# Two chained MLPs after a DFT on one Trainium2 core: operands shifted by 32 bytes, PSUM pools kept across the change of stage, the last flush and the last product done differently

## Chip, core and metric

One NeuronCore of a Trainium2 chip (trn2). The metric is the device time of one execution in microseconds, smaller is better. TensorE is called PE here, its weight loads PEld, VectorE DVE, ScalarE ACT, GpSimd POOL, SyncE SP.

## What is computed

```python
X = np.fft.fft(np.fft.fft(x, axis=1), axis=2).real        # x: 4 x 3072 x 256, float32
h = X.reshape(-1, 256) @ w_in                              # 12288 x 2048
y = np.maximum(0.01 * h, h) @ w_out                        # first MLP, 12288 x 256
y_prev = y shifted by one token inside each batch
xk = mu_k * y + (1 - mu_k) * y_prev;  xr = the same with mu_r
k = np.maximum(xk @ w_k, 0.0)                              # 12288 x 1024
out = sigmoid(xr @ w_r) * ((k * k) @ w_v)                  # second MLP
```

The weights arrive as float64 and are split on the chip. Precision is kept by writing each operand as a high part and a low part in `fp32r` and adding three products, high x high, high x low and low x high: so one mathematical matmul is three on PE.

## The kernel before

**Two stages.** The tokens are cut into 24 tiles of 512 (4 batches, 2 halves by symmetry of the DFT, 3 tiles each). The first stage does, for every batch, the DFT along the sequence by cosine and sine tables (`fft_mm`, line 309) and the first MLP; the DFT along the 256 columns is folded into `w_in` at the start (line 401). Its results `y` go to DRAM. The second stage reads them back as `xa` and, shifted by one token, `xb` (`load_tile`, line 671) and does the second MLP, tile after tile. The order of all work is written out by hand: each engine runs its instructions in the order in which the Python code issues them.

**First MLP.** For each of 16 slices `u` of the 2048 hidden columns (`step`, line 592) PE does 3 matmuls `mm_b` (line 508), 3 `mm_a` for the next slice (line 496), both into a PSUM tile of pool `ps_s` (tag `s`, 4 banks), and 12 matmuls `outmm` (line 519) into the four banks of pool `ps_o` (tags `o00` to `o11`): 18 matmuls of 128x128 stationary and 512 moving columns per slice. At the last slice of a tile `flush` (line 522) copies the four banks on ACT into two SBUF tiles `yo` of pool `work` and sends each to DRAM.

**The change of stage (lines 942 to 963).** The first two hidden slices of tile 0 of the second MLP are computed early out of `stage` tiles. Then the pools `work`, `pqp`, `mv`, `wp` (SBUF) and `ps_o`, `ps_s` (PSUM) are released, and `p2` (SBUF) and `ps2` (PSUM) take their space. The first user of a place in a new pool waits for everything that still uses the old pool there.

**Second MLP (lines 1014 to 1054).** For each tile and each of 8 hidden slices `f`: 6 matmuls `kps` (line 932), relu on ACT (`rl`, line 936), square on DVE (line 937), split into `k2h` and `k2l`, and two slices later 6 matmuls `v` (line 975) into two banks. In two of the slices 6 matmuls `rps` (line 983) feed the sigmoid. So a tile has 8 x 6 + 8 x 6 + 2 x 6 = 108 matmuls. Meanwhile the operands of the next tile are made: `mt` on ACT (line 688), `mx` on DVE (line 689), then the split `mh` (ACT, line 128) and `ml` (DVE, line 135). These six steps begin at slice `f1` of the tile before, one step per slice:

```python
        f0, f1, g0 = (0, 2, 4) if ti else (2, 5, 5)
```

At the end of a tile `finish` (line 987) multiplies gate and `v` on DVE and stores the two halves `m`; for the last tile each half is stored by itself.

**Where the operands lie.** All pools start on fixed byte offsets inside a partition of SBUF; every matmul's moving operand is a row of 512 x 4 = 2048 bytes there, its stationary operand a row of 512 bytes. `w2p` (the second MLP's weights) is allocated from the right end, `wp`, `mv`, `p2` and others from the left, after `misc`. As the built program places them, the start addresses modulo 64 bytes are:

```
matmuls                       moving operand        stationary operand     moving, stationary mod 64
first MLP, o (line 519)       gh 93056, gl 117632   uoh 76672, uol 84864   0, 0
first MLP, ps (496, 508)      Ph 101248, Qh 109440  wh 43904, wl 60288     0, 0
second MLP, kps (932)         mh 109504, ml 117696  wkh 192480             0, 32
second MLP, v (975)           k2h 64448, k2l 70592  wvh 208864             0, 32
second MLP, tile 0, kps       mh 20608 (in stage)   wkh 192480             0, 32
DFT (309)                     tables from 201568    sh 222176, sl 223712   0, 8, 32, 40, 48, 56; 32
dps (540), 2 weight columns   wh, wl                dcs 43520 or 43552     0, 0 or 32
```

Of the kernel before, what the change touches and what calls it, by code (L numbers as in the profile page):

```python
# [9 lines left out]
F32 = mybir.dt.float32  # L10
# [3 lines left out]
ALU = mybir.AluOpType  # L14
PSUM = bass.MemoryType.PSUM
DRAM = bass.MemoryType.DRAM

P = 128
B = 4
# [6 lines left out]
NK = FK // P  # L26
J = 384
JP = 386
W = 512
NT = M // W  # L30
# [72 lines left out]
def fft_mlp_kernel(ctx, tc, xs, x7, x8, x87, tb, tbs, alt, ce, so, mu, w_in, w_out, w_k, w_v, w_r, out):  # L103
    nc = tc.nc
    ctx.enter_context(tc.manual_schedule())
    V, A, T, G, Q = nc.vector, nc.scalar, nc.tensor, nc.gpsimd, nc.sync

    dram = ctx.enter_context(tc.tile_pool(name="dram", bufs=1, space=DRAM))
    yd = [[dram.tile([P, 2, M], F32, name=f"y{b}_{s}") for s in range(2)] for b in range(B)]
# [4 lines left out]
    ps_s = tc.alloc_tile_pool(name="ps_s", bufs=4, space=PSUM)  # L114
    ps_o = tc.alloc_tile_pool(name="ps_o", bufs=1, space=PSUM)
    stage = ctx.enter_context(tc.tile_pool(name="stage", bufs=3))
    misc = ctx.enter_context(tc.tile_pool(name="misc", bufs=1))
    x87t = misc.tile([1, 2, 4], F32, name="x87t")
    w128 = misc.tile([P, NF], F32, name="w128")
    wp = tc.alloc_tile_pool(name="wp", bufs=1)  # L120

    mv = tc.alloc_tile_pool(name="mv", bufs=1)
# [397 lines left out]
                     start=(u == 0 and i == 0), stop=(u == NF - 1 and i == 2))  # L520

    def flush(b, t, po):
        for s in range(2):
            yo = work.tile([P, 2, W], F32, tag="yo", bufs=2, name="yo")
            for h in range(2):
                act_copy(yo[:, h], po[s][h])
            Q.dma_start(yd[b][s][:, :, t * W:(t + 1) * W], yo)
# [136 lines left out]
    for n in range(len(sources)):  # L664
        a, c = w2_piece(n)
# [288 lines left out]
    pqp.release()  # L954
    mv.release()
    wp.release()
    ps_o.release()
    ps_s.release()


    ps2 = ctx.enter_context(tc.tile_pool(name="ps2", bufs=1, space=PSUM))
    p2 = w2["p2"] = ctx.enter_context(tc.tile_pool(name="p2", bufs=2))
    p2.tile([P, 16], F32, tag="pad", bufs=1, name="pad3")

    NB = D // P

    def v_mm(f, kk, vps):
        hi, lo = kk
        ws = ((w2["vh"], hi), (w2["vl"], hi), (w2["vh"], lo))
        order = [(i, m) for i in range(3) for m in range(NB)]  # L970
        if f == NK - 1:
            order = [(i, m) for m in range(NB) for i in range(3)]
        for i, m in order:
            w, x = ws[i]
            T.matmul(vps[m], w[:, f, m * P:(m + 1) * P], x, start=(f == 0 and i == 0), stop=(f == NK - 1 and i == 2))  # L975

    def r_mm(xr, sig, m):
        hi, lo = xr
        ps = ps2.tile([P, 512], F32, tag="rps", bufs=2, name="rps")
        i = 0  # L980
        for w, x in ((w2["rh"], hi), (w2["rl"], hi), (w2["rh"], lo)):
            for k in range(2):
                T.matmul(ps, w[:, k, m * P:(m + 1) * P], x[:, k], start=(i == 0), stop=(i == 5))  # L983
                i += 1
        A.activation(sig[:, m], ps, ACTF.Sigmoid)

    def finish(ti, vps, sig):
        o = p2.tile([P, NB, W], F32, tag="o", name="o")
        for m in range(NB):
            V.tensor_tensor(o[:, m], sig[:, m], vps[m], op=ALU.mult)  # L990
            if ti == len(tiles) - 1:
                Q.dma_start(out[ti, :, m], o[:, m])
        if ti < len(tiles) - 1:
            Q.dma_start(out[ti], o)

# [6 lines left out]
    def drain():  # L1002
        if q2:
            t, f, kk = q2.pop(0)
            if f == 0:
                t["v"] = [ps2.tile([P, 512], F32, tag="v", bufs=4, name=f"v{m}") for m in range(NB)]
            v_mm(f, kk, t["v"])
            if f == NK - 1:
                finish(t["i"], t["v"], t["sig"])

# [4 lines left out]
    for ti in range(len(tiles)):  # L1015
        rd = ready.pop(ti)
        t = {"i": ti, "sig": p2.tile([P, NB, W], F32, tag="sig", name="sig")}
        end = ti == len(tiles) - 1
        f0, f1, g0 = (0, 2, 4) if ti else (2, 5, 5)
        if ti == 0:  # L1020
            q1.append((t, 1, early[1][2]))
            q2.append((t, 0, kk0))
        for f in range(f0, NK):
            ps = ps2.tile([P, 512], F32, tag="k", bufs=2, name="kps")
            r = p2.tile([P, W], F32, tag="r", bufs=3, name="rl")
            k2 = p2.tile([P, W], F32, tag="k2", bufs=3, name="k2")
            k_mm(ps, f, rd["k"])
            k_ev(ps, r, k2)
            if q1:
                tt, ff, kk2 = q1.pop(0)  # L1030
                q2.append((tt, ff, k_split(kk2)))
            q1.append((t, f, k2))
            t["rk"] = rd.get("r")
            if not end and g0 <= f < g0 + NB:
                gate(t, f - g0)
            if end and f == NK - 1:
                gate(t, 0)
            if len(q2) > 1:
                drain()
            if f == f0:  # L1040
                for n in ((1, 2) if ti == 0 else (ti + 2,)):
                    if n < len(tiles):
                        loaded[n] = load_tile(n)
            if f == f1 and not end:
                for g in todo:
                    g()
                todo = do_prep(ti + 1)
            if todo:
                todo.pop(0)()
# [4 lines left out]
    drain()  # L1054
    for k in ("xp", "pool"):
        w2[k].release()


def dft_tables():
# [73 lines left out]
```

## Time and profile before

| | |
|---|---|
| median of 3 runs | 1498.52 us (1498.14 to 1502.74) |
| the profiled execution, its own time | 1498.63 us |
| its span, first to last instruction | 1496.9 us |
| PE busy | 1479.1 us, 99% of the span |
| PEld busy | 1203.2 us, 80% |
| DVE busy | 1008.2 us, 67% |
| ACT busy | 893.0 us, 60% |
| POOL busy | 124.2 us, 8% |
| granted TensorE clock | full (2.4 GHz) in all 40 slices of the span |

The profiled execution took 1.7 us more than its span. Matmuls overlap in the pipe, so the time that a matmul is listed with (390 ns) is its passage and not what it costs: what it costs is the distance from its start to the next start. A busy share of 99% for PE therefore says that PE always had something in flight, not that it ran at its peak.

### The profile page before, as it was taken

The page shows a single profiled execution, that of the slowest core. Times are in us where ns is not written, and L with a number is a line of the kernel's source. Part 1 is how long each engine was busy: PE and PEld are TensorE (multiplying, and loading weights), DVE is VectorE, ACT ScalarE, POOL GpSimd, SP SyncE. Part 2 cuts the span into 40 slices and gives each one's busy share as a digit, 9 for nine tenths or more (in the row PEclk, how much of TensorE's full clock was granted, in tenths as well). Part 3 has the DMA queues.
Part 4 walks back from the last instruction along what each step waited for, and adds up shares of the span by engine and source line. Part 5 has one row for each costly group of instructions (what it writes and reads, how often), then busy time and mean ns, then how long its engine had stood idle before and what let it go on. Part 6 is the DMA issues. An engine that isn't in the chain of part 4 may idle for free.

```text
span 1496.9 us, 17655 instructions
## 1 busy us (share of the span) xinstructions
PE 1479.1 (99%) x6460; PEld 1203.2 (80%) x6460; DVE 1008.2 (67%) x1409; ACT 893.0 (60%) x1473; POOL 124.2 (8%) x145
## 2 busy tenths in 40 slices
PE   6999999999999999999999999999999999999998
PEld 3788888888888888888888877888888888888887
DVE  7886767666666766676767656666666666666664
ACT  4776566565665665665666656555555555555563
POOL 2333000222000221000000000000000000000000
PEclk9999999999999999999999999999999999999999
DMA  8767132654141751232220111212121212121200
GB/s 318 216 180 131 32 114 91 203 111 83 36 156 62 200 99 36 68 124 92 89 68 0 57 64 64 85 42 85 43 84 43 85 43 78 50 71 57 71 29 29
DMA packets 88449, 134.23 MB, mean 90 GB/s; under 512 B 31342, under 2 KB 51575, under 8 KB 84778
## 3 DMA queue, kind: packets, MB, share of 16 engines
q1 hardware_dynamic: 73098, 86.50, 18.1%
q0 software_dynamic: 15264, 46.60, 12.6%
q8 instruction: 50, 0.82, 0.2%
q14 instruction: 37, 0.30, 0.1%
HBM read 105.20 MB, written 27.89 MB: 89 GB/s over the span
## 4 chain that ended last, share of the span: by engine, by line
PE 98%; DVE 1%; DMA 0%; ACT 0%; issue 0%; SPq 0%; POOL 0%; POOLq 0%; DVEq 0%; ACTq 0%
PE o L519 35%; PE v L975 18%; PE kps L932 18%; PE ps L508 9%; PE ps L496 9%; PE rps L983 4%; PE wps L401 1%; PE dps L540 1%; PE cps L450 0%; DMA cet<-in_ce 0%; PE f0Po L309 0%; PE f0Pe L309 0%; PE f3Pe L309 0%; PE f2Pe L309 0%; PE f0Qe L309 0%
## 5 line engine op out<-in xcount | busy, mean ns | idle before, releaser
L579 DVE SCALAR_TENSOR_TENSOR g<-ev,ps 128x512 f32<-128x512 f32 x192 | 131.7, 686 | 191.9 <-PE ps L508 191.3
L936 ACT ACTIVATE rl<-kps 128x512 f32<-128x512 f32 x190 | 113.6, 598 | 245.1 <-PE kps L932 241.7
L937 DVE SCALAR_TENSOR_TENSOR k<-kps,rl 128x512 f32<-128x512 f32 x190 | 131.3, 691 | 163.2 <-ACT rl L936 160.9
L567 DVE TENSOR_TENSOR gl<-g,gh 128x1024 fp32r<-128x1024 f32 x192 | 235.1, 1224 | 4.5 <-ACT gh L128 4.5
L128 ACT ACTIVATE gh<-g 128x1024 fp32r<-128x1024 f32 x192 | 202.7, 1056 | 51.6 <-PE o L519 49.8
L519 PE MATMUL o<-gh,uoh 128*128 128x512 f32 x768 | 212.0, 390 | 1.0 <-ACT gh L128 1.0
L519 PE MATMUL o<-gl,uoh 128*128 128x512 f32 x768 | 211.3, 389 | 0.0
L519 PE MATMUL o<-gh,uol 128*128 128x512 f32 x768 | 211.1, 389 | 0.0
L131 ACT ACTIVATE g<-ps 128x512 f32<-128x512 f32 x192 | 114.4, 596 | 150.2 <-DVE g L579 149.2
L519 PEld LDWEIGHTS o<-gh,uoh 128*128 128x128 f32 x768 | 144.1, 188 | 31.9 <-ACT gh L128 1.5
L519 PEld LDWEIGHTS o<-gl,uoh 128*128 128x128 f32 x768 | 144.1, 188 | 30.2 <-DVE gl L567 0.3
L519 PEld LDWEIGHTS o<-gh,uol 128*128 128x128 f32 x768 | 144.1, 188 | 30.1
L501 DVE SCALAR_TENSOR_TENSOR ev<-cb,w,ps 128x512 f32<-128x512 f32 x192 | 143.1, 746 | 4.4 <-PE ps L496 2.6
L135 DVE TENSOR_TENSOR k2l<-k,k2h 128x512 fp32r<-128x512 f32 x190 | 129.1, 680 | 0.6 <-ACT k2h L128 0.6
L975 PE MATMUL v<-k2h,wvh 128*128 128x512 f32 x382 | 123.9, 396 | 0.0
L975 PE MATMUL v<-k2h,wvl 128*128 128x512 f32 x382 | 123.8, 396 | 0.0
L975 PE MATMUL v<-k2l,wvh 128*128 128x512 f32 x382 | 123.8, 396 | 0.0
L131 ACT ACTIVATE g<-g 128x512 f32<-128x512 f32 x192 | 119.8, 624 | 2.2 <-DVE g L579 2.2
L932 PE MATMUL kps<-mh,wkh 128*128 128x512 f32 x380 | 119.4, 396 | 1.5 <-ACT mh L128 0.8
L932 PE MATMUL kps<-ml,wkh 128*128 128x512 f32 x380 | 119.4, 396 | 0.1
L932 PE MATMUL kps<-mh,wkl 128*128 128x512 f32 x380 | 119.3, 395 | 0.0
L128 ACT ACTIVATE k2h<-k 128x512 fp32r<-128x512 f32 x190 | 119.1, 627 | 0.0
(395 smaller groups left out, 2183.0 us busy)
## 6 DMA issues: line engine op xcount, KB each, us to landing
y<-yo SPq DMA_DIRECT2D x24, 512.0 KB
xa<-y SPq DMA_DIRECT2D x24, 512.0 KB
out_dram<-o SPq DMA_DIRECT2D x23, 512.0 KB
tab_a<-in_tbs POOLq DMA_DIRECT2D x8, 1158.0 KB, 6.1
tab_b<-in_tbs POOLq DMA_DIRECT2D x8, 1158.0 KB, 5.8
tab_c<-in_tbs POOLq DMA_DIRECT2D x6, 1158.0 KB, 6.3
tab_d<-in_tbs POOLq DMA_DIRECT2D x6, 1158.0 KB, 6.4
pm<-in_xs POOLq DMA_DIRECT2D x54, 128.0 KB, 3.1
```

The lines of the kernel that those rows point to most:

```text
L128: A.activation(o, i, ACTF.Copy)
L131: A.activation(o, i, ACTF.Prelu, alpha=0.01)
L135: V.tensor_tensor(lo, src, hi.bitcast(F32), op=ALU.subtract)
L496: T.matmul(x["ps"], l[:, f], r, start=(i == 0), stop=(i == 2))
L501: V.scalar_tensor_tensor(x["ev"], x["cb"], w128[:, u:u + 1], x["ps"], op0=ALU.mult, op1=ALU.add)
L508: T.matmul(x["ps"], l[:, f], r, start=False, stop=(i == 2), skip_group_check=True)
L519: T.matmul(po[s][h], w[:, u % HF, h * P:(h + 1) * P], g[:, s], start=(u == 0 and i == 0), stop=(u == NF - 1 and i == 2))
L567: V.tensor_tensor(gl, x["g"], x["gh"].bitcast(F32), op=ALU.subtract)
L579: V.scalar_tensor_tensor(x["gt"][:, 1], x["ev"], 2.0, x["ps"], op0=ALU.mult, op1=ALU.subtract)
L932: T.matmul(ps, w[:, k, sl], x[:, k], start=(i == 0), stop=(i == 5))
L937: V.scalar_tensor_tensor(k2, ps, 0.0, r, op0=ALU.max, op1=ALU.mult)
L975: T.matmul(vps[m], w[:, f, m * P:(m + 1) * P], x, start=(f == 0 and i == 0), stop=(f == NK - 1 and i == 2))
```

## The change

Five edits:

- A tile `padm` of 32 bytes in pool `misc`. What is allocated from the left after it moves by 32 bytes: `wp`, `mv`, `pqp`, `work`, `p2` (a few `misc` tiles too). `stage`, and what is allocated from the right (the tables, `sh`, `sl`, the second MLP's weights), stay.
- `ps_s` and `ps_o` are no longer released; `kps` and `rps` take tag `s` of `ps_s` (4 banks for both), `v` takes tags `o00`, `o01` in even tiles and `o10`, `o11` in odd ones. Before, `kps` and `rps` had 2 banks each and `v` 4.
- The last flush (`b == B - 1`, last tile) stages its first half in a `stage` tile of tag `st`, and its second half in two `stage` tiles of tag `h` with a store each, and not in `work`.
- `f1` of tile 0 goes from 5 to 4.
- In the last tile, the last `v` bank is finished in two halves of 256 columns (6 matmuls of 256 columns instead of 3 of 512), each multiplied and stored by itself.

```diff
+    misc.tile([P, 8], F32, name="padm")
     wp = tc.alloc_tile_pool(name="wp", bufs=1)
...
     def flush(b, t, po):
+        end = b == B - 1 and t == NT - 1
         for s in range(2):
+            if end:
+                at = yd[b][s][:, :, t * W:(t + 1) * W]
+                yo = stage.tile([P, 2, W], F32, tag="st", bufs=3, name="yo") if s == 0 else None
+                for h in range(2):
+                    half = yo[:, h] if s == 0 else stage.tile([P, W], F32, tag="h", bufs=2, name="yh")
+                    act_copy(half, po[s][h])
+                    if s:
+                        Q.dma_start(at[:, h], half)
+                if s == 0:
+                    Q.dma_start(at, yo)
+                continue
...
-    ps_o.release()
-    ps_s.release()
-
-
-    ps2 = ctx.enter_context(tc.tile_pool(name="ps2", bufs=1, space=PSUM))
...
         if f == NK - 1:
-            order = [(i, m) for m in range(NB) for i in range(3)]
+            halves = [slice(0, W // 2), slice(W // 2, W)] if end else [slice(0, W)]
+            order = [(i, m, c) for m in range(NB) for c in (halves if m == NB - 1 else [slice(0, W)]) for i in range(3)]
...
-        ps = ps2.tile([P, 512], F32, tag="rps", bufs=2, name="rps")
+        ps = ps_s.tile([P, 512], F32, tag="s", name="rps")
...
-                t["v"] = [ps2.tile([P, 512], F32, tag="v", bufs=4, name=f"v{m}") for m in range(NB)]
+                t["v"] = [ps_o.tile([P, 512], F32, tag=f"o{t['i'] % 2}{m}", name=f"v{m}") for m in range(NB)]
...
-        f0, f1, g0 = (0, 2, 4) if ti else (2, 5, 5)
+        f0, f1, g0 = (0, 2, 4) if ti else (2, 4, 5)
...
-            ps = ps2.tile([P, 512], F32, tag="k", bufs=2, name="kps")
+            ps = ps_s.tile([P, 512], F32, tag="s", name="kps")
```

With the pad the addresses modulo 64 of moving and stationary operand become 32, 32 in the first MLP and 32, 32 in the second; tile 0's `kps`, the DFT and `dps` keep the relation that they had.

**What moves, on ACT after the change of stage.** Before, from tile 0's `mh` for the gate to tile 1's `mh` (`mt_7632` and `mh_7688` belong to tile 1):

```order
L128 ACTIVATE mh_7599<-mx_7552 128x1024
L936 ACTIVATE rl_7604<-kps_7603 128x512
L128 ACTIVATE k2h_7614<-k2_7580 128x512
L985 ACT_TABLE_LOAD
L985 ACTIVATE sig_7517<-rps_7618 128x512
L688 ACTIVATE mt_7632<-xb_7542,omu_114 128x512
L936 ACTIVATE rl_7637<-kps_7636 128x512
L128 ACTIVATE k2h_7647<-k2_7605 128x512
L985 ACTIVATE sig_7517<-rps_7651 128x512
L688 ACTIVATE mt_7632<-xb_7542,omu_114 128x512
L936 ACTIVATE rl_7668<-kps_7667 128x512
...
L128 ACTIVATE mh_7688<-mx_7633 128x1024
```

And now (`mt_7601` and `mh_7665` belong to tile 1):

```order
L129 ACTIVATE mh_7597<-mx_7550 128x1024
L701 ACTIVATE mt_7601<-xb_7540,omu_115 128x512
L949 ACTIVATE rl_7606<-kps_7605 128x512
L129 ACTIVATE k2h_7616<-k2_7578 128x512
L997 ACT_TABLE_LOAD
L997 ACTIVATE sig_7515<-rps_7620 128x512
L701 ACTIVATE mt_7601<-xb_7540,omu_115 128x512
L949 ACTIVATE rl_7637<-kps_7636 128x512
L129 ACTIVATE k2h_7647<-k2_7607 128x512
L997 ACTIVATE sig_7515<-rps_7651 128x512
L129 ACTIVATE mh_7665<-mx_7602 128x1024
```

All three steps of tile 1 stand one hidden slice earlier: the first `mt` ahead of the `rl` of slice 5, and `mh` ahead of the `rl` of slice 7.

**On SP, the last flush and the loads of tile 1.** In brackets stand the semaphores waited for (`DMAHW` of transfers, `PE`, `DVE`, `Activation` of engines). Before:

```order
L527 DMA y3_0_65<-yo_7495 256x1x512 [waits DMAHW4_49,Activation_49]
L527 DMA y3_1_66<-yo_7499 256x1x512 [waits DMAHW5_49,Activation_49]
L677 DMA xa_7541<-y0_0_59 128x2x512 [waits DMAHW5_49,DMAHW4_49,DMAHW6_49,DVE_49,PE_49]
L682 DMA xb_7542<-y0_0_59 128x2x255 [waits DMAHW7_49]
L682 DMA xb_7542<-y0_0_59 128x2x1 [waits DMAHW0_49]
```

And now:

```order
L535 DMA y3_0_65<-yo_7496 256x1x512 [waits DMAHW4_49,Activation_49]
L533 DMA y3_1_66<-yh_7500 128x512 [waits DMAHW5_49,Activation_49]
L533 DMA y3_1_66<-yh_7503 128x512 [waits DMAHW6_49,Activation_49]
L690 DMA xa_7539<-y0_0_59 128x2x512 [waits DMAHW7_49,DVE_49,PE_49]
L695 DMA xb_7540<-y0_0_59 128x2x255 [waits DMAHW0_49]
```

There is one store more ahead of the load `xa`, and `xa` no longer waits for the transfers of the stores (`DMAHW4`, `DMAHW5`, which were the two `yo` just above it); `PE` is the last matmul of the first MLP.

**On PE, the last matmuls of the program.** Before:

```order
L975 MATMUL v_12526<-k2l,wvh 128x512
L975 MATMUL v_12527<-k2h,wvh 128x512
L975 MATMUL v_12527<-k2h,wvl 128x512
L975 MATMUL v_12527<-k2l,wvh 128x512
L1126 UNCONDITIONAL_BRANCH
```

And now:

```order
L986 MATMUL v_12524<-k2l,wvh 128x512
L986 MATMUL v_12525<-k2h,wvh 128x256
L986 MATMUL v_12525<-k2h,wvl 128x256
L986 MATMUL v_12525<-k2l,wvh 128x256
L986 MATMUL v_12525<-k2h,wvh 128x256
L986 MATMUL v_12525<-k2h,wvl 128x256
L986 MATMUL v_12525<-k2l,wvh 128x256
L1142 UNCONDITIONAL_BRANCH
```

Three matmuls, and three loads of weights with them, are more. Nowhere else does PE's order change.

## Rows read from the trace of the kernel before

**Rows 1.** The page: the chain that ended last, by engine.

```profile
PE 98%; DVE 1%; DMA 0%; ACT 0%; issue 0%; SPq 0%; POOL 0%; POOLq 0%; DVEq 0%; ACTq 0%
```

**Rows 2.** Busy time by window, with PEclk, DMA share, GB/s last.

```profile
552.00:608.00 56.00, 56.00 (x249) 46.37 (x248) 38.38 (x49) 31.31 (x46) 9.06 (x11) 1.00 0.25 40
920.00:1490.00 570.00, 570.00 (x2444) 458.87 (x2443) 375.25 (x544) 325.17 (x540) 0.00 (x0) 1.00 0.18 61
```

**Rows 3.** Timeline: start us, us, engine, line, what, count; both stages.

```profile
555.10 0.39 PE L508 MATMUL ps<-Qh,wh 128*128 128x512 f32 x1
...
608.14 0.39 PE L508 MATMUL ps<-Qh,wh 128*128 128x512 f32 x1
...
992.37 1.28 DVE L990 TENSOR_TENSOR o<-sig,v 128x512 f32<-128x512 f32 x2
...
1471.17 1.28 DVE L990 TENSOR_TENSOR o<-sig,v 128x512 f32<-128x512 f32 x2
```

**Rows 4.** Matmuls by line and shape: count | busy us, mean ns.

```profile
L519 PE MATMUL o<-gh,uol 128*128 128x512 f32 x768 | 211.1, 389 | 0.0
...
L932 PE MATMUL kps<-mh,wkl 128*128 128x512 f32 x380 | 119.3, 395 | 0.0
...
L540 PE MATMUL dps<-wl,dcs 128*2 128x512 f32 x16 | 6.4, 397 | 0.0
...
L309 PE MATMUL f2Pe<-tab_b,sh2Pe 128*128 128x386 f32 x6 | 1.5, 340 | 0.0
```

**Rows 5.** Timeline of PE: tile 0's early slice inside the first stage.

```profile
880.05 0.62 PE L932 MATMUL ps<-mh,wkh 128*128 128x512 f32 x2
...
881.45 1.07 PE L519 MATMUL o<-gh,uoh 128*128 128x512 f32 x4
```

**Rows 6.** Timeline of PE: first MLP, right behind a DFT block.

```profile
500.24 0.40 PE L508 MATMUL ps<-Ql,wh 128*128 128x512 f32 x1
...
501.17 0.39 PE L496 MATMUL ps<-Ph,wl 128*128 128x512 f32 x1
```

**Rows 7.** Timeline of PE through the change of stage; idle time in brackets.

```profile
888.08 0.39 PE L519 MATMUL o<-gl,uoh 128*128 128x512 f32 x1
...
889.15 0.72 PE L932 MATMUL kps<-mh,wkh 128*128 128x512 f32 x2 [0.69 <-ACT yo L128]
...
890.65 0.63 PE L975 MATMUL v<-er,wvh 128*128 128x512 f32 x2
...
908.60 0.63 PE L975 MATMUL v<-k2l,wvh 128*128 128x512 f32 x2
...
910.04 0.73 PE L932 MATMUL kps<-mh,wkh 128*128 128x512 f32 x2 [0.81 <-ACT mh L128]
...
911.88 0.63 PE L975 MATMUL v<-k2h,wvh 128*128 128x512 f32 x2
```

**Rows 8.** Timeline of ACT and SP there.

```profile
886.79 2.30 ACT L128 ACTIVATE yo<-o 128x512 f32<-128x512 f32 x4
...
892.35 0.57 SPq L677 DMA_DIRECT2D xa<-y  x1
892.38 0.60 ACT L936 ACTIVATE rl<-kps 128x512 f32<-128x512 f32 x1 [3.28 <-DMA y<-yo]
...
902.43 0.71 ACT L688 ACTIVATE mt<-xb,omu 128x512 f32<-128x512 f32 x1
...
908.94 1.05 ACT L128 ACTIVATE mh<-mx 128x1024 fp32r<-128x1024 f32 x1
```

**Rows 9.** Timeline of the end; a half-wide DVE operation; DMA over 1490 to 1500.

```profile
1492.37 1.46 DVE L990 TENSOR_TENSOR o<-sig,v 128x512 f32<-128x512 f32 x2 [3.06 <-PE v L975]
...
1493.09 1.10 SPq L992 DMA_DIRECT2D out_dram<-o  x2
...
L232 DVE TENSOR_TENSOR pm<-xl 128x256 f32<-128x256 f32 x18 | 7.5, 419 | 0.0
...
GB/s 0 0 0 0 0 0 0 0 0 0 0 0 0 0 0 82 401 385 238 377 385 230 0 0 0 0 0 0 0 0 0 0 0 0 0 0 0 0 0 0
```

More of the change, by code (lines that the diff above doesn't have):

```diff
@@ L965, in fft_mlp_kernel, with v_mm @@
     NB = D // P
-    def v_mm(f, kk, vps):
+    def v_mm(f, kk, vps, end):
         hi, lo = kk
         ws = ((w2["vh"], hi), (w2["vl"], hi), (w2["vh"], lo))
-        order = [(i, m) for i in range(3) for m in range(NB)]
+        order = [(i, m, slice(0, W)) for i in range(3) for m in range(NB)]
         if f == NK - 1:
-            order = [(i, m) for m in range(NB) for i in range(3)]
-        for i, m in order:
+            halves = [slice(0, W // 2), slice(W // 2, W)] if end else [slice(0, W)]
+            order = [(i, m, c) for m in range(NB) for c in (halves if m == NB - 1 else [slice(0, W)]) for i in range(3)]
+        for i, m, c in order:
             w, x = ws[i]
-            T.matmul(vps[m], w[:, f, m * P:(m + 1) * P], x, start=(f == 0 and i == 0), stop=(f == NK - 1 and i == 2))
+            T.matmul(vps[m][:, c], w[:, f, m * P:(m + 1) * P], x[:, c], start=(f == 0 and i == 0),
+                     stop=(f == NK - 1 and i == 2), skip_group_check=c.start > 0)
     def r_mm(xr, sig, m):
         hi, lo = xr
-        ps = ps2.tile([P, 512], F32, tag="rps", bufs=2, name="rps")
+        ps = ps_s.tile([P, 512], F32, tag="s", name="rps")
         i = 0
@@ L988, in finish @@
         o = p2.tile([P, NB, W], F32, tag="o", name="o")
+        end = ti == len(tiles) - 1
         for m in range(NB):
-            V.tensor_tensor(o[:, m], sig[:, m], vps[m], op=ALU.mult)
-            if ti == len(tiles) - 1:
-                Q.dma_start(out[ti, :, m], o[:, m])
+            for c in [slice(0, W // 2), slice(W // 2, W)] if end and m == NB - 1 else [slice(0, W)]:
+                V.tensor_tensor(o[:, m, c], sig[:, m, c], vps[m][:, c], op=ALU.mult)
+                if end:
+                    Q.dma_start(out[ti, :, m, c], o[:, m, c])
         if ti < len(tiles) - 1:
@@ L1005, in drain @@
             if f == 0:
-                t["v"] = [ps2.tile([P, 512], F32, tag="v", bufs=4, name=f"v{m}") for m in range(NB)]
-            v_mm(f, kk, t["v"])
+                t["v"] = [ps_o.tile([P, 512], F32, tag=f"o{t['i'] % 2}{m}", name=f"v{m}") for m in range(NB)]
+            v_mm(f, kk, t["v"], t["i"] == len(tiles) - 1)
             if f == NK - 1:
@@ L1056, in fft_mlp_kernel @@
         w2[k].release()
+    ps_o.release()
+    ps_s.release()
 def dft_tables():
```

## Prediction

> **What bounds the kernel now.** I read the chain of waits on the profile's page first: 98% of the span is PE, and next to nothing waits for a transfer or for another engine [rows 1]. So two things can make the kernel shorter: fewer or faster matmuls, and the few places where PE stops. Next the busy time by window, for the clock: it is 1.00 in the first stage and in the second, so both run at the 2.4 GHz level, and in the second DVE works 375 of 570 us and ACT 325: neither is near a limit [rows 2]. Then the timeline, for what one matmul costs. In the first MLP, `ps` at 555.10 and `ps` at 608.14 stand 13 slices apart: 53.04 us over 13 x 18 = 234 matmuls are **226.7 ns** each. In the second, the products at 992.37 and 1471.17 stand 19 tiles apart: 478.80 us over 19 x 108 = 2052 matmuls are **233.3 ns** [rows 3]. Both stream 512 columns, which is 213.3 ns at 2.4 GHz. The reader should see that the same form of matmul costs 6.67 ns more in one stage than in the other, with nothing waiting.
>
> What can that come from? The list by line shows the two paces as two durations, 389 ns for `o` and 395 for `kps` [rows 4]. The program offers three differences: the order of PSUM banks, the code around, and the place of the operands modulo 64 bytes (0 and 0 in the first MLP, 0 and 32 in the second). One place separates them. Tile 0's early `ps<-mh,wkh` stands inside the first stage, among `o` matmuls, with six matmuls into one bank of the first MLP's own pool; its operands lie at 0 and 32. From its start at 880.05 to the next `o` at 881.45 its six matmuls take 1.40 us, 233 ns each [rows 5]. So the slow pace goes with the operands and not with the stage or the pool. What remains is whether it is the distance between the two operands or the stationary one's own offset. The DFT has its stationary operand always at 32 and its moving one at several offsets; its 386 columns stream in 160.8 ns and are listed with 340, a rest of 179 ns, where `o` has 389 - 213 = 176 and `kps` 395 - 213 = 182 [rows 4]. A stationary operand at 32 thus doesn't by itself cost the full 182. I read this, with no more than moderate confidence, as the distance. Against it stands `dps`, with two columns of weights, half of them at the moving operand's offset: 397 ns in the mean [rows 4].
>
> **The pad.** In the changed program moving and stationary operand agree modulo 64 in both stages, 32 and 32; no instruction is added. First MLP: the two still agree, so I cost it at nothing. Second MLP: 23 of the 24 tiles get what the first MLP has; tile 0 does not, since its `mh` lies in `stage`, which is not moved, and its other matmuls stand among these. 23 x 108 = 2484 matmuls x 6.67 ns = **16.6 us**, all of it on the path. The bounds: no gain at all (the pace stays at 233.3), and no row of a 512-column matmul that is faster than 226.7, so not more than this, save some 0.7 us for tile 0 (108 x 6.67 ns). I take the upper end, because the nearest rows are those of the same shape with the same relation of offsets. With a tile at 108 x 226.7 ns = 24.5 us, DVE's 375/570 of the present 25.2 us is 16.6 us and ACT's 325/570 is 14.4: both stay covered by PE.
>
> The Trainium skill speaks against this term: TensorE: Matmul & The Clock Gate (Step-by-step: what each phase is for) says that PE has two independent read ports on SBUF, one for the moving operand and one for the weight load, so that loading the next weights takes nothing from the running matmul. By that rule it doesn't matter where the two lie, and the pad's term is 0 instead of 16.6. The Trainium skill's TensorE: Matmul & The Clock Gate (Back-to-back issue gap) gives about 216 ns for 512 columns; neither pace of this trace agrees with it, and the measured ones decide.
>
> **PSUM pools kept, last flush staged elsewhere.** Before, the first `kps` waits for ACT's copies of the four `o` banks, because its new pool waits for the old ones: PE idles 0.69 us before 889.15. From the `o` at 888.08 to the `v` at 890.65 seven matmuls take 2.57 us, and at pace they take 0.23 + 6 x 0.233 = 1.63: **0.94 us** is lost, the restart of the pipe included [rows 7]. In the changed program `kps` takes a bank of `ps_s` that has been free for long, and `v` needs only the first two of the four copies. These start at 886.79 and take 2.30/4 = 0.58 us each, so they end at about 887.95 [rows 8]; `v` comes six matmuls after 888.31, at 889.7. So the 0.94 us goes, and nothing takes its place. `kps` and `rps` share four banks instead of two and two: not fewer. ACT's `rl` waited 3.28 us for the transfer of `yo` [rows 8]; that wait goes too, and PE gains little by it, as `v` stands two slices behind. The extra store on SP stands ahead of `xa`; the two stores at the end of the program take 1.10 us to issue, 0.55 each [rows 9]. ACT's fourth copy ends at 889.1, so `xa` can issue at about 889.1 + 0.55 = 889.7 instead of 892.35 [rows 8]: 2.6 us earlier, with the extra store counted.
>
> **`f1` from 5 to 4.** Tile 1's first `kps` starts late, since `mh` comes late: ACT begins it at 908.94 and needs 1.05 us, PE idles 0.81 us before 910.04 [rows 7, 8]. From 908.60 to 911.88, 8 matmuls take 3.28 us and at pace 8 x 0.233 = 1.87: **1.41 us** is lost [rows 7]. Moved up by one slice (18 matmuls with the gate's in it, 4.2 us), `mh` ends at about 909.99 - 4.2 = 905.8, less what PE gains upstream; PE asks for it at 908.60 + 2 x 0.233 = 909.07, less the 0.94. That is some 2.3 us of slack, and the 1.41 us goes. The new risk is the first `mt`: from 902.43 it moves to about 898, and needs `xa` and `xb` in SBUF. These were issued from 892.35 on and now from 889.7 on, so their lead over `mt` is 8 us instead of 10. ACT's `rl` and `k2h` of slice 5 stand 0.71 us later behind it, which `v`'s two slices of lag cover; without that cover PE would lose those 0.71 us once.
>
> **The last product.** Before, DVE does its two products from 1492.37 to 1493.83; the second store issues in the second half of the 1.10 us from 1493.09 [rows 9]. Now the second product is two: between 0.345 us each (half of the 0.69 of `1.46` with its gap) and 0.69; the nearest row is a 256-wide operation at 419 ns [rows 9], so I take 0.42. DVE then ends at 1493.08 + 2 x 0.42 + 0.02 = 1493.94, 0.1 us later. PE's six half matmuls cost between 107 ns (their columns) and 233 ns; at 233 the last ends 0.7 us later and the second product begins at about 1493.8, for an end at 1494.2. The last transfer is half as large: 256 KB at the 385 GB/s of the slices in which the last stores move [rows 9] takes 0.68 us, so it saves about 0.34. The sum lies between -0.3 and +0.1; I take **-0.2**.
>
> **The sum**, against the profiled execution's own 1498.63 us, which is 0.1 above the median of the runs: 1498.63 - 16.6 - 0.94 - 1.41 - 0.2 = **1479.5 us**.
>
> **Rivals.**
>
> *The pad does nothing.* The pace is no matter of distance, or it settles at 233 for any operands that don't start at a multiple of 64. For it: the first MLP too runs at the slow pace for a while behind a DFT block, four matmuls in 0.93 us from 500.24 [rows 6], so the pace is partly a state and not a property of a pair; and `dps`. Against it: rows 5, and that each stage holds its pace over hundreds of microseconds. Then only the waits go: 1498.63 - 2.55 = 1496.1 us. By the Trainium skill's two read ports (TensorE: Matmul & The Clock Gate, Step-by-step: what each phase is for) it would come out this way too.
>
> *The stationary operand's own offset decides* (the other side). A weight load that starts at 32 instead of 0 costs 6.67 ns, whatever the moving operand does. Then the second MLP gains nothing, for its weights are not moved, and the first MLP's matmuls lie at 32 now. These are 4 batches x 3 pairs of tiles x 16 slices x 18 = 3456; x 6.67 ns = 23 us more. 1498.63 + 23 - 2.55 = 1519 us. For it: all slow `kps` and `v` have weights at 32. Against it: the DFT's rest of 179 ns [rows 4]. It decides as soon as the first MLP's pace rises by over 0.7 ns (2.55 us over 3456), if the second's stays.
>
> *The loads of tile 1 come late.* They share the DMA engines with the flush, and `mt` asks earlier; then up to the old 1.41 us stays: 1480.9 us, inside the forecast.
>
> **How the numbers follow.** The forecast has a chance of 0.77, a partial gain of the pad included (half of it gives 1487.8); no effect of the pad 0.12; a slower first MLP 0.11. About 0.3%, 4.5 us, is what a measurement of this kernel can tell from no change: the waits alone, 2.55 us, are below that. So faster 0.77, same 0.12, slower 0.11. The range runs from 1478, where tile 0 gains too and the end saves a little more, to 1497, which takes in the case without the pad's effect; the slower case is left out. The forecast's own range is 1478 to 1488.
>
> **What would show it.** Right: `kps` and `v` at 389 ns instead of 395, products of successive tiles 24.5 us apart instead of 25.2, `o` still at 389, no bracket before the first `kps` of tile 0 and of tile 1, and a span of about 1477.8. Wrong: `o` at 395 (the second rival), `kps` at 395 (the first), or a new bracket on ACT's `mt` waiting for `xb`.

## The result and the profile after

| | before | changed |
|---|---|---|
| median | 1498.71 us (4 runs) | **1480.48 us** (4 runs, 1480.32 to 1480.61) |
| ratio to before | | 0.9873, 95% interval 0.9855 to 0.9890 |
| span of the profiled execution | 1496.9 us | 1478.8 us |

The forecast was 1479.5 us, in a range of 1478.0 to 1497.0. The page of the changed kernel, its span and the chain that ended last by engine: PE still ends everything, as in [rows 1].

```profile
span 1478.8 us, 17665 instructions
...
PE 98%; DVE 1%; DMA 0%; ACT 0%; issue 0%; SPq 0%; POOL 0%; POOLq 0%; DVEq 0%; ACTq 0%
```

The pace first. Matmuls of the changed kernel by line and shape (count, busy us, mean ns), to set beside [rows 4]; then its timeline of PE and DVE at the places of [rows 3].

```profile
L520 PE MATMUL o<-gh,uol 128*128 128x512 f32 x768 | 211.1, 389 | 0.0
L986 PE MATMUL v<-k2l,wvh 128*128 128x512 f32 x381 | 121.1, 389 | 0.0
...
L945 PE MATMUL kps<-mh,wkl 128*128 128x512 f32 x380 | 117.0, 389 | 0.0
```

```profile
555.95 0.39 PE L509 MATMUL ps<-Qh,wh 128*128 128x512 f32 x1
...
608.99 0.39 PE L509 MATMUL ps<-Qh,wh 128*128 128x512 f32 x1
...
988.27 1.28 DVE L1004 TENSOR_TENSOR o<-sig,v 128x512 f32<-128x512 f32 x2
...
1453.39 1.28 DVE L1004 TENSOR_TENSOR o<-sig,v 128x512 f32<-128x512 f32 x2
```

`kps` and `v` are listed with 389 ns instead of 395 or 396, as `o` always was. The first MLP takes the same 53.04 us for its 13 slices, so its pace is untouched by the shift to 32, 32. In the second MLP 19 tiles take 465.12 us instead of 478.80: 2052 matmuls at 226.7 ns instead of 233.3. This alone is 13.68 us of the 18.1 that the span lost.

Then the change of stage, on PE:

```profile
888.93 0.39 PE L520 MATMUL o<-gl,uoh 128*128 128x512 f32 x1
889.15 0.63 PE L945 MATMUL kps<-mh,wkh 128*128 128x512 f32 x2
...
890.56 0.63 PE L986 MATMUL v<-er,wvh 128*128 128x512 f32 x2
...
908.17 0.63 PE L986 MATMUL v<-k2l,wvh 128*128 128x512 f32 x2
908.64 0.62 PE L945 MATMUL kps<-mh,wkh 128*128 128x512 f32 x2
```

Both brackets of [rows 7] are gone. From the `o` at 888.93 to the `v` at 890.56 seven matmuls take 1.63 us (2.57 before), and tile 1's first `kps` at 908.64 stands two matmuls behind the `v` at 908.17. Between these two places, from `v` at 890.56 to `v` at 908.17, tile 0 takes 17.61 us, and took 17.95 before (890.65 to 908.60): 0.34 us that the prediction did not have. On ACT, tile 1's `mh` is done at 906.21, 2.4 us before PE asks for it:

```profile
905.16 1.05 ACT L129 ACTIVATE mh<-mx 128x1024 fp32r<-128x1024 f32 x1
```

The end, on DVE and SP:

```profile
1473.93 1.53 DVE L1004 TENSOR_TENSOR o<-sig,v 128x512 f32<-128x512 f32 x3 [2.92 <-PE v L986]
1474.65 1.35 SPq L1006 DMA_DIRECT2D out_dram<-o  x3
```

From the first product's start to the end of the span it is 4.87 us now, and was 1496.9 - 1492.37 = 4.53 [rows 9]: 0.34 us **more**. DVE's products end 0.07 us later against their start (1.53 for 1.46), and SP has issued its third store 2.07 us after the first product began, where the second was issued after 1.82. But the bytes do not leave later. What the DMA engines moved, in GB/s, over 1471 to 1479 in slices of 0.2 us, to set beside [rows 9]:

```profile
GB/s 0 0 0 0 0 0 0 0 0 0 0 0 0 0 0 0 0 0 0 0 0 0 225 369 410 333 312 359 343 266 5 0 0 0 0 0 0 0 0 0
```

Both kernels store the same 0.52 MB without a pause. By the DMA records of the kept traces the last data packet ends at 1477.06, 3.13 us behind the start of the first product; before, it ended at 1495.54, 3.17 us behind it. The loss lies behind the data: from there to the last instruction it is 1.77 us now and was 1.32. At the end SP waits for the semaphores of the transfers one after another, and each wait takes about 0.06 us. Before, one wait stood behind that for the last store: it was over at 1495.90, the list at 1496.03. Now seven stand behind it: it is over at 1477.52, the list at 1478.01. That is 0.36 us of the 0.45; the other 0.09 lie between the last packet and that wait. No run changed this order by itself.

The beginning cost something too. PE in the first microseconds, before and then changed:

```profile
12.97 2.11 PE L450 MATMUL cps<-tab_c,c8m 128*4 128x386 f32 x6
```

```profile
12.75 2.96 PE L451 MATMUL cps<-tab_c,c8m 128*4 128x386 f32 x6
```

The same six matmuls took 0.85 us longer in the changed kernel's profiled execution. The pad moves their weights `c8m` by 32 bytes, but that is not it: both lengths occur with the pad and without it (with it 2.11 to 2.96 us in the profiled executions, without it 2.11 to 2.90). It is the clock. The views print 1.00 from the start, but the kept traces hold the granted clock as records with a start, and the first record, at the full level (2.4 GHz), starts at 12.93 us before and only at 14.51 us in the changed kernel. Ahead of it there is no record, and the matmuls go at half the pace: four `wps` take 1.84 us from 9.06 and 0.97 from 15.64. So no record names the level there; the pace is that of the lower one, 1.2 GHz. PE had worked without a pause from 9.29 and 9.06 on when it rose. At half pace up to the record the six matmuls should lose half of 14.51 - 12.75, which is 0.88 us; they lost 0.85. The same sum gives the length of these six within 0.03 us in all 14 kept traces. The page before, with its full clock in all 40 slices, doesn't show this.

The first stage ends later by the same 0.85 us, the last `o` at 888.93 for 888.08, but that is partly chance: the first matmul started 0.22 us earlier, and another 0.24 us were lost at 39 us, where the third group of `o` matmuls waits for DVE's `gl` (39.68 for 38.82) behind a transfer for which DVE waited 0.33 us.

So the 18.1 us add up, by the rows above: 0.85 lost by the end of the first stage; 18.44 + 0.85 = 19.29 won from there to the first of the last products (from 1492.37 to 1473.93 is 18.44); 0.34 lost at the end. Of the 19.29, 0.94 lie between `o` and the first `v`, 0.34 in tile 0, and 18.01 behind it, which is 16.6 + 1.41.

### The profile page after: what moved, and what is told of

The parts are those of the page before. It is cut to its first block, busy times and chain, and to the rows that moved or that the text cites. A ratio compares the mean times of both kernels' runs of the same rounds, so it can differ in the third digit from the quotient of the medians.

```text
span 1478.8 us, 17665 instructions
## 1 busy us (share of the span) xinstructions
PE 1462.4 (99%) x6463; PEld 1203.6 (81%) x6463; DVE 1008.7 (68%) x1410; ACT 892.6 (60%) x1473; POOL 124.0 (8%) x145
## 4 chain that ended last, share of the span: by engine, by line
PE 98%; DVE 1%; ACT 0%; DMA 0%; issue 0%; SPq 0%; POOL 0%; DVEq 0%; POOLq 0%; ACTq 0%
PE o L520 35%; PE v L986 18%; PE kps L945 17%; PE ps L497 9%; PE ps L509 9%; PE rps L995 4%; PE wps L402 1%; PE cps L451 1%; PE dps L553 1%; DMA cet<-in_ce 0%; PE f0Po L310 0%; PE f0Pe L310 0%; PE f2Pe L310 0%; PE f1Pe L310 0%; PE f0Qe L310 0%; PE f3Pe L310 0%
```

## The experiments

Distances below are the start of the moving operand minus that of the stationary one, modulo 512 bytes, as the built programs place them: 0 in the first MLP before and after, 480 in the second before and 0 after, 160 in both for what tile 0 reads from `stage` (its `ps`, its `kps` and its first `v`). The median of the kernel before lay between 1498.9 and 1499.2 us beside these runs.

**The pad alone, in the kernel before.**

```diff
     w128 = misc.tile([P, NF], F32, name="w128")
+    misc.tile([P, 8], F32, name="padm")
```

> The kernel before plus the 32-byte pad and nothing else: PSUM pools, last flush, f1 and last product as before. Theory D (the distance of moving and stationary operand modulo 64 sets the pace): products of successive tiles of the second MLP 24.48 us apart instead of 25.2, first MLP still 226.7 ns, both brackets at the change of stage still there: 1498.7 - 16.6 = about 1482.1 us. Rival P (the shared PSUM pools, four banks for kps and rps, make the second MLP's pace): kps and v stay at 233.3 ns, about 1498.7 us.

Measured: 1483.1 us, ratio 0.9892 (0.9878 to 0.9907). Products on DVE, and the two waits on PE, which are still there:

```profile
990.93 1.28 DVE L991 TENSOR_TENSOR o<-sig,v 128x512 f32<-128x512 f32 x2
...
1456.05 1.28 DVE L991 TENSOR_TENSOR o<-sig,v 128x512 f32<-128x512 f32 x2
```

```profile
889.92 0.73 PE L933 MATMUL kps<-mh,wkh 128*128 128x512 f32 x2 [0.69 <-ACT yo L129]
...
910.82 0.73 PE L933 MATMUL kps<-mh,wkh 128*128 128x512 f32 x2 [0.82 <-ACT mh L129]
```

19 tiles in 465.12 us: the pad by itself makes the whole new pace, with the old PSUM pools. Rival P falls.

**The change without the pad.**

```diff
-    misc.tile([P, 8], F32, name="padm")
```

> The changed kernel without the pad, all else as changed. Theory D: the second MLP is back at 233.3 ns, the gain at the change of stage stays: 1480.5 + 16.6 = about 1497.1 us. Rival P: the pace of 226.7 stays, 1480.5 us within 0.5.

Measured: 1497.74 us, ratio 0.9990 (0.9980 to 1.0000).

```profile
991.49 1.28 DVE L1003 TENSOR_TENSOR o<-sig,v 128x512 f32<-128x512 f32 x2
...
1470.29 1.28 DVE L1003 TENSOR_TENSOR o<-sig,v 128x512 f32<-128x512 f32 x2
```

478.80 us for 19 tiles, the old pace. What is left, the four other edits together, is worth 1.4 us and can hardly be told from nothing by the run's time. In the trace it can: no bracket is left at the change of stage, and though the last `o` starts at 889.77, 1.69 us later than before, the span is 0.5 us shorter. So about 2.2 us are won behind it, where 0.94 + 1.41 - 0.34 = 2.0 were to be expected. Tile 0 between its two places here:

```profile
891.40 0.63 PE L985 MATMUL v<-er,wvh 128*128 128x512 f32 x2
...
909.13 0.63 PE L985 MATMUL v<-k2l,wvh 128*128 128x512 f32 x2
```

That is 17.73 us, for 17.95 before and 17.61 in the changed kernel. So of tile 0's 0.34 us the waits make 0.22 and the pad 0.12: tile 0's `rps` and most of its `v` read moving operands from `p2`, which the pad moves.

**The weights moved instead of the moving operands.** The kernel before, with 32 bytes behind the second MLP's weights, which pushes them 32 bytes down.

```diff
                 w2[nm + x] = w2p.tile([P, k, f], F32R, name=f"w{nm}{x}")
+        w2p.tile([P, 8], F32, name="padr")
```

> The kernel before, with 32 bytes at the other end: the second MLP's weights lie 32 bytes lower, so moving and stationary operand are at 0 and 0 modulo 64, and tile 0's mh in stage agrees with them modulo 64 too (though not modulo 128 to 512: 192 apart). Theory D: 24 x 108 matmuls at 226.7 ns, tile 0 included, 1498.7 - 17.3 = about 1481.4 us. Rival M (a moving operand at 32 is what is fast in the second MLP, wherever the weights lie): stays at 233.3, about 1498.7 us. If tile 0 alone stays at 233 ns, the modulus is larger than 64.

Measured: 1482.7 us, ratio 0.9890 (0.9876 to 0.9905). Products on DVE, and tile 0's `kps` by line between 880 and 904 us:

```profile
991.91 1.28 DVE L991 TENSOR_TENSOR o<-sig,v 128x512 f32<-128x512 f32 x2
...
1457.03 1.28 DVE L991 TENSOR_TENSOR o<-sig,v 128x512 f32<-128x512 f32 x2
```

```profile
L933 PE MATMUL kps<-mh,wkl 128*128 128x512 f32 x8 | 2.5, 396 | 0.0
```

465.12 us again: with moving and stationary operand at 0 and 0 the pace is that of 32 and 32. But tile 0, whose two operands also agree modulo 64 here (distance 192), stays at 396 ns. So the modulus is not 64, unless tile 0's pace has another cause (the last experiment settles that).

**Both moved.** The changed kernel with the same `padr`: moving at 32, stationary at 0, distance 32.

> The changed kernel with the second MLP's weights 32 bytes lower as well: moving at 32, stationary at 0. Theory D: the pace is 233.3 ns again in tiles 1 to 23, with tile 0's kps at 226.7: 1480.5 + 16.6 - 0.3 = about 1496.8 us. Rival M (moving operand at 32 is enough) or rival S (a stationary operand at 0 is enough): 226.7, about 1480.5 us.

Measured: 1497.68 us, ratio 0.9988 (0.9979 to 0.9997).

```profile
990.41 1.28 DVE L1005 TENSOR_TENSOR o<-sig,v 128x512 f32<-128x512 f32 x2
...
1444.01 1.28 DVE L1005 TENSOR_TENSOR o<-sig,v 128x512 f32<-128x512 f32 x2
```

18 tiles in 453.60 us, 25.2 each: slow. Neither operand's own place decides, rivals M and S fall; the distance does. That tile 0 would be fast was wrong, as in the run before.

**64 bytes apart.**

```diff
-    p2.tile([P, 16], F32, tag="pad", bufs=1, name="pad3")
+    p2.tile([P, 32], F32, tag="pad", bufs=1, name="pad3")
```

> The changed kernel with the second MLP's moving operands 64 bytes further: moving and stationary operand agree modulo 64, no longer modulo 128. Theory D64 (modulus 64): no change, 226.7 ns, 1480.5 us within 1. Rival D128 (modulus 128 or more): 233.3 ns in tiles 1 to 23, about 1497.1 us.

Measured: 1485.43 us, ratio 0.9905 (0.9890 to 0.9920).

```profile
988.38 1.28 DVE L1004 TENSOR_TENSOR o<-sig,v 128x512 f32<-128x512 f32 x2
...
1458.06 1.28 DVE L1004 TENSOR_TENSOR o<-sig,v 128x512 f32<-128x512 f32 x2
```

Both theories fall: 469.68 us for 19 tiles is 228.9 ns a matmul, a third pace. It is a mean: by the starts in the kept trace about a third of the matmuls follow at 225 or 226 ns, the others at 229 to 232. 2484 matmuls by 2.2 ns more are 5.5 us; the run is 5.0 us longer than the changed kernel.

**Half of the first MLP's second-layer weights off.**

```diff
     pqp = tc.alloc_tile_pool(name="pqp", bufs=1)
+    pqp.tile([P, 8], F32, name="padq")
```

> The changed kernel with half of the first MLP's second-layer weights 32 bytes off, so that 8 of every 16 slices have o at 32 and 0 and the others at 32 and 32: 1152 of 3456 matmuls. Theory D: these 1152 take 233.3 ns, the others of the same stage 226.7: 12 o matmuls 2.80 us instead of 2.72 in alternating blocks of 8 slices, 1480.5 + 7.7 = about 1488.2 us. If the pace were a state of the stage that a few aligned matmuls hold up or break: all at 226.7, 1480.5 us, or all at 233.3, about 1503 us.

Measured: 1488.52 us, ratio 0.9928 (0.9909 to 0.9947), 8.0 us over the changed kernel where 7.7 were expected. PE over slices on either side of the change from aligned to shifted weights:

```profile
576.46 0.39 PE L510 MATMUL ps<-Qh,wh 128*128 128x512 f32 x1
...
580.54 0.39 PE L510 MATMUL ps<-Qh,wh 128*128 128x512 f32 x1
...
588.78 0.39 PE L510 MATMUL ps<-Qh,wh 128*128 128x512 f32 x1
...
592.95 0.39 PE L510 MATMUL ps<-Qh,wh 128*128 128x512 f32 x1
```

An aligned slice takes 4.08 us and a shifted one 4.17. The pace follows the operands from one slice to the next, in the stage that was always fast. It is a property of the matmuls, and not of the stage.

One row says that it may not be a property of a matmul's own two operands. The shifted weights are those of `o` alone; `ps` has both its operands at distance 0 throughout. The last `ps` ahead of the `o`, in the aligned slice above and in the shifted one:

```profile
577.59 0.39 PE L498 MATMUL ps<-Ph,wl 128*128 128x512 f32 x1
...
589.92 0.40 PE L498 MATMUL ps<-Ph,wl 128*128 128x512 f32 x1
```

In the mean of six slices it is listed with 389 ns in aligned ones (560 to 584 us) and with 397, as a slow matmul is, in shifted ones (588 to 613 us), where it runs just ahead of the first shifted weights. So the weights that count may be those of the next matmul, loaded while this one runs. Against that stands that the slow pace outlasts the shifted weights too: the `ps` behind the last `o` is listed with 393. In the other runs all weights of a stretch agree modulo 512, and none of them can tell the two apart; this is not settled.

**Two new distances per kernel.** 128 in the first MLP and 256 in the second; then 384 and 448. The first kernel's edit (384 and 448 likewise):

```diff
     mv = tc.alloc_tile_pool(name="mv", bufs=1)
+    mv.tile([P, 32], F32, name="padv")
...
-        wo.tile([P, 80], F32, name="pad2")
+        wo.tile([P, 48], F32, name="pad2")
...
-    p2.tile([P, 16], F32, tag="pad", bufs=1, name="pad3")
+    p2.tile([P, 80], F32, tag="pad", bufs=1, name="pad3")
```

> The changed kernel with two new distances, counted modulo 512 as moving minus stationary: 128 in the first MLP, 256 in the second. So far: 0 gives 226.7 ns, 64 gives 228.9, 32, 160, 192 and 480 give 233 to 233.5. Theory N (distance 0 alone is best; other multiples of 64 lie between 226.7 and 233.5): at 228.9 in both, 3456 x 2.2 + 2484 x 2.2 = 13 us more, about 1493.6 us; at 233.3 in both, 1480.5 + 23 + 16.6 = 1520 us. Rival L (some other distance is faster than 0, as the DFT's short rests suggest): under 1480.5 us.

> The same with 384 in the first MLP and 448 in the second. Theory N: 1480 to 1520 us, at 228.9 in both about 1493.6. Rival L: the DFT, whose distances are 384 to 448 and so on, has the shortest rest there, and one of the two stages is faster than 226.7 ns: under 1480.5 us for that stage's part.

Measured: 1501.27 us, ratio 1.0014 (1.0004 to 1.0023), and 1517.79 us, ratio 1.0126 (1.0109 to 1.0143). One slice of the first MLP and 19 tiles of the second, at 128 and 256:

```profile
563.54 0.40 PE L510 MATMUL ps<-Qh,wh 128*128 128x512 f32 x1
...
567.74 0.40 PE L510 MATMUL ps<-Qh,wh 128*128 128x512 f32 x1
```

```profile
1008.78 1.28 DVE L1005 TENSOR_TENSOR o<-sig,v 128x512 f32<-128x512 f32 x2
...
1473.90 1.28 DVE L1005 TENSOR_TENSOR o<-sig,v 128x512 f32<-128x512 f32 x2
```

And at 384 and 448:

```profile
562.74 0.40 PE L510 MATMUL ps<-Qh,wh 128*128 128x512 f32 x1
...
566.94 0.40 PE L510 MATMUL ps<-Qh,wh 128*128 128x512 f32 x1
```

```profile
985.17 1.28 DVE L1005 TENSOR_TENSOR o<-sig,v 128x512 f32<-128x512 f32 x2
...
1463.97 1.28 DVE L1005 TENSOR_TENSOR o<-sig,v 128x512 f32<-128x512 f32 x2
```

The first MLP's slice takes 4.20 us, 18 matmuls at 233.3 ns, at 128 and at 384. The second MLP has 465.12 us at 256, as fast as at 0, and 478.80 at 448. So the stages have changed places in the first kernel: the same `o` that was fast in the kernel before is slow, and `kps` is fast at an offset that no earlier kernel had. Two fast distances, 0 and 256, and the same pace at 128 and 384 and at 192 and 448: within what was tried, the distance counts modulo 256. The first kernel is 20.8 us longer than the changed one, not the 23 that 3456 matmuls give: about 230 of them, most of them behind DFT blocks as in [rows 6], are slow in the changed kernel already.

| distance modulo 256 | pace, ns | where |
|---|---|---|
| 0 | 226.7 | first MLP, changed second MLP; 256 in the second MLP |
| 32 | 233.3 | second MLP, both moved |
| 64 | 228.9 in the mean | second MLP, 64 apart |
| 128 | 233.3 | first MLP at 128 and at 384 |
| 192 | 233.3 | second MLP at 448 |
| 224 | 233.3 | second MLP before (480) |

Tile 0 stays slow at 160 (before and changed) and at 192. Distance 96 was not tried with a full matmul. No distance tried gave less than 226.7 ns: rival L falls.

**`f1` back to 5.**

```diff
-        f0, f1, g0 = (0, 2, 4) if ti else (2, 4, 5)
+        f0, f1, g0 = (0, 2, 4) if ti else (2, 5, 5)
```

> The changed kernel with f1 of tile 0 back at 5, all else as changed. The prediction's term: tile 1's mh is late again and PE waits for it before tile 1's first kps, 1.41 us over eight matmuls: 1480.5 + 1.4 = about 1481.9 us, with that bracket back in the timeline and the first one (before tile 0's kps) still gone. Rival: the earlier load of xa is what did it, and mh comes in time with f1 at 5 as well: no bracket, 1480.5 us.

Measured: 1481.32 us, ratio 0.9885 (0.9868 to 0.9901).

```profile
907.15 0.63 PE L986 MATMUL v<-k2l,wvh 128*128 128x512 f32 x2
908.60 0.73 PE L945 MATMUL kps<-mh,wkh 128*128 128x512 f32 x2 [0.82 <-ACT mh L129]
...
910.43 0.62 PE L986 MATMUL v<-k2h,wvh 128*128 128x512 f32 x2
```

The bracket is back, and eight matmuls take 3.28 us, exactly as before the change [rows 7]. The earlier `xa` didn't cure it; the slice did. By the run's time it is 0.8 us instead of 1.4. The start covers the rest: here the last `o` starts at 887.91, 1.02 us earlier than in the changed kernel, and the span is 0.5 us longer, so 1.5 us are lost behind it.

**The last product in one piece.**

```diff
-            halves = [slice(0, W // 2), slice(W // 2, W)] if end else [slice(0, W)]
+            halves = [slice(0, W)]
...
-            for c in [slice(0, W // 2), slice(W // 2, W)] if end and m == NB - 1 else [slice(0, W)]:
+            for c in [slice(0, W)]:
```

> The changed kernel with the last product in one piece, as before. As the prediction sized it, the halves save 0.2 us: then 1480.7 us. As the trace of the changed kernel reads (from the first product's start to the span's end 4.88 us instead of 4.46), they cost 0.4 us: then 1480.1 us, with two stores at the end and two late semaphore waits behind them.

Measured: 1479.40 us, ratio 0.9866 (0.9851 to 0.9881), span 1478.1.

```profile
1473.72 1.44 DVE L1004 TENSOR_TENSOR o<-sig,v 128x512 f32<-128x512 f32 x2 [2.92 <-PE v L986]
```

From the first product to the end 1478.1 - 1473.72 = 4.38 us instead of 4.87: the halves cost 0.5 us here. The last data packet ends 3.15 us behind the first product's start, with the halves 3.13; from there to the last instruction it is 1.26 us instead of 1.77. So it is again what stands behind the data, and here no wait for a transfer stands behind that for the last store. The runs agree (1479.21 to 1479.90, against 1480.32 to 1480.61), though the two intervals of the ratios overlap.

**The best parts together.** No pad, `padr` as above (all at 0 and 0), last product in one piece; and the same with all distances at 0, tile 0's too. The edit of the second (the first has `[P, 8]` in `padr` and leaves `pad3` as it was; both have the edit of the run above as well):

```diff
-    misc.tile([P, 8], F32, name="padm")
...
+        w2p.tile([P, 88], F32, name="padr")
...
-    p2.tile([P, 16], F32, tag="pad", bufs=1, name="pad3")
+    p2.tile([P, 64], F32, tag="pad", bufs=1, name="pad3")
```

> The best parts together: the changed kernel with no pad, the second MLP's weights 32 bytes lower (moving and stationary at 0 and 0 modulo 64 in both stages and in tile 0 too), and the last product in one piece. Theory D: tile 0 gains 0.3 to 0.7 us, the end 0.4: 1480.5 - 0.9 = about 1479.6 us. If tile 0 gains nothing and the end neither, 1480.5 us.

> The changed kernel without the pad; the second MLP's weights 352 bytes lower and its moving operands 192 higher, so that all 512-column matmuls of both MLPs, tile 0's early ones too, have distance 0 modulo 512; last product in one piece. Theory N: tile 0's 54 kps and early ps matmuls and the v among them at 226.7 instead of 233.5 and 229: 0.4 to 0.7 us below the version with the last product in one piece alone (1479.4): about 1478.9 us. If tile 0's pace has another cause (its transition, its other pool): 1479.4 us.

Measured: 1479.68 us, ratio 0.9867 (0.9852 to 0.9883), and 1480.02 us, ratio 0.9870 (0.9856 to 0.9885). The first is no faster than the changed kernel with one piece, for tile 0 has distance 192 in it and gains nothing. Tile 0's early slice on PE, in the first and then in the second:

```profile
879.90 0.63 PE L945 MATMUL ps<-mh,wkh 128*128 128x512 f32 x2
...
881.30 1.09 PE L519 MATMUL o<-gh,uoh 128*128 128x512 f32 x4
```

```profile
882.22 0.61 PE L945 MATMUL ps<-mh,wkh 128*128 128x512 f32 x2
...
883.58 1.07 PE L519 MATMUL o<-gh,uoh 128*128 128x512 f32 x4
```

At distance 0 the six matmuls take 1.36 us instead of 1.40, 227 ns each instead of 233. So tile 0's pace too was the distance. In the trace the second kernel reaches this slice 2.32 us later than the first and the last products only 1.87 us later (1474.79 for 1472.92): 0.45 us won, where 54 matmuls at 6.67 ns are 0.36. It doesn't show in the run's time, for this kernel's profiled execution lost 1.39 us at its start, behind a transfer that came late to DVE:

```profile
38.09 1.40 DVE L501 SCALAR_TENSOR_TENSOR ev<-cb,w,ps 128x512 f32<-128x512 f32 x2 [1.62 <-DMA w<-rd]
...
41.01 1.19 PE L519 MATMUL o<-gl,uoh 128*128 128x512 f32 x4 [1.39 <-DVE gl L579]
```

Its four runs spread over 2.7 us (1478.24 to 1480.96). Of the versions tried the changed kernel with the last product in one piece had the lowest median, 1.1 us below the changed kernel and 0.3 to 0.6 below these two, which is less than their starts vary.

## Why the prediction was right, point by point

**The pad, 16.6 us: right.** The measured pace is the forecast one, 226.7 ns in tiles 1 to 23, the first MLP unchanged, and 18.01 us won behind tile 0 for the 16.6 + 1.41 of the sum. Between its two places tile 0 gained 0.12 us by the pad, since only its `kps` and its first `v` keep their old distance; the prediction gave it nothing. The reason given, the distance between the operands, is shown by six runs: moving either operand alone makes the pace, moving both unmakes it, and it can be taken from the first MLP by the half or whole. Whether the stationary operand that counts is the matmul's own or the next one's is open. What was wrong is its modulus. The prediction argued with offsets modulo 64; the runs say 256. It did no harm because the pad makes the distance exactly 0, and that was luck: agreement modulo 64 alone would have left 228.9 ns at 64 and 233.3 at 128. The table of addresses had a hint: every fast line in it is at a distance of 0 modulo 512. And `dps`, which the prediction held against itself as "half of them at the moving operand's offset", never was aligned: its distances by that table, 43904 - 43520 and 60288 - 43552, are 128 and 96 modulo 256. A row that speaks against a theory may be speaking against its modulus.

**The inference that spoke against the pad: it did not hold.** By the Trainium skill's TensorE: Matmul & The Clock Gate (Step-by-step: what each phase is for), PE has two independent read ports, and loading the next weights takes no read bandwidth from the running matmul. The prediction drew from it that the place of the operands would not matter. The runs differ: the same 18 matmuls of a slice take 4.08 or 4.20 us by nothing but the distance of their operands. What in the chip meets there no run here shows.

**PSUM pools and last flush, 0.94 us: right.** Seven matmuls in 1.63 us, the number that the prediction had for them at pace. Which of the two edits does it no run tells, since none has one without the other. That ACT's wait for the transfer of `yo` goes too was said to gain PE little. The 0.22 us of tile 0 is where it can have gone: before, PE takes 0.55 us for two matmuls from 893.00 and 0.56 for the next two, where 0.47 is the pace. No run has this alone.

**`f1`, 1.41 us: right.** The wait is gone, it is back alone when the edit is undone, and `mh` is early by 2.4 us where 2.3 were forecast.

**The last product, -0.2 us: wrong in sign.** It cost 0.3 to 0.5. The step that failed is "The last transfer is half as large [...] so it saves about 0.34". Both kernels move the same 0.52 MB back to back, so the last byte leaves 3.13 us behind the first product for 3.17 before, however the stores are cut. What the prediction left out is what stands behind the data, 1.77 us for 1.32: with the halves seven of SP's waits stand behind that for the last store instead of one, and that is 0.36 us of it.

**The sum, 1.0 us too low.** The profiled execution took 1480.61 us, 1.11 over the 1479.5. 0.85 of it was lost by the end of the first stage, in the main by the clock, and 0.54 at the end (0.34 lost for 0.2 won); the 0.34 of tile 0 is on the other side. The sum set out from one execution of the kernel before whose clock rose early: what it missed at the start is chance, and so is that it didn't miss by more.

**The rivals.** "The pad does nothing" and "the stationary operand's own offset decides" both fall: the first MLP runs at 226.7 with its weights at 32. The slow start behind a DFT block, held for the first rival, is there in the changed kernel too; it was not studied further.

## What to carry to other kernels

Where a long row of equal matmuls runs at two paces in two stages with nothing waiting, compare the start addresses of moving and stationary operand before anything else: here a pad of 32 bytes was worth 16.6 us of 1498, and a wrong distance in the first MLP cost 20.8. Take the distance to exactly 0, not to a modulus that a few rows suggest, and count every pool that the pad pushes along. Cutting the last store in two wins nothing where all the stores leave back to back; look at when the last byte leaves and at what stands behind it. And read the first microseconds for the clock, by the pace of equal matmuls, before a difference of one microsecond is put down to an edit.

## What the runs showed of the hardware that was not expected

The cost of one 512-column matmul with its own load of weights depends on where its operands lie towards each other. The mean paces found are 226.7, 228.9 and 233.3 ns, and among the distances tried they repeat after 256 bytes. The slowest is 2.9% above the fastest.

The first microseconds of the program vary by about one microsecond from run to run. The full clock is on record from 12.7 to 15.4 us on in the kept traces, and the matmuls ahead of that go at half pace (2.11 or 2.96 us for the same six). DVE's wait for the same transfer at 37 us is 0.3 or 1.6 us. So edits worth less than that have to be read in their own place in the trace and not in the time of the run.

Once the last bytes have left, the end of the program took 1.26 to 1.77 us, the longer the more of SP's waits stand behind that for the last store (none, one, seven: 1.26, 1.32, 1.77).
